# Strided attention output transposed per channel chunk and copied by ScalarE; strided jobs cut by slice halves; w_in issued behind batch 0's loads; attention steps at other places

## The chip, the cores and the metric

The kernel runs on one core of a Trainium2 chip. The metric is the time of one execution in microseconds (us) on the device. Engines are named as in the profile: PE is TensorE (PEld its weight loads), DVE VectorE, ACT ScalarE, POOL GpSimd, SP SyncE, whose queue issues most DMAs here.

## The reference

A sparse attention over 8 batches, 8 heads, 576 tokens and 64 channels, then a two-layer product with the Mish activation over all 4608 tokens.

```python
scores = q @ k^T / 8                       # per batch and head
heads 0..3: keys 0 to 31 places back       # "local"
heads 4..7: keys back in steps of 32       # "strided"
x = softmax(masked scores) @ v             # 4608 x 512, head by head in its columns
h = x @ w_in                               # 512 -> 2048
g = h * tanh(log(1 + exp(h)))              # Mish
out = g @ w_out                            # 2048 -> 512, float32
```

## The kernel before

**Layout of the attention.** Local heads work on six windows of 96 queries with 128 keys each. For strided heads a batch's tokens are laid out as 72 rows p of 8 slices j (token = 8p + j), so that a slice's 72 tokens hold all keys that its queries may see; a small mask, `stm`, selects them. After the products, x_l (local, 96 x 6 x 256) and x_s (strided, 72 x 8 x 256) are transposed on PE into xT, which has channels on partitions in four chunks of 128 (0 and 1 local, 2 and 3 strided) and the tokens of four batches in its columns, as a ring.

**Steps of a batch.** Eight t steps transpose q and k (`t_step`; each is 6 or 8 PE transposes into PSUM and one copy out, to qTs, kTs, qTl, kTl). Eight qk steps (`qk`, four strided and four local) put scores for two heads into the PSUM tile `ps`; ACT takes the exponential into a tile P, and POOL or DVE multiplies the mask on. Fourteen pv steps (`pv`, eight strided, one for each slice, six local, one for each window) multiply P with v for four heads into the PSUM tile `po`; DVE takes the reciprocal of the sums (`rden`) and multiplies it on, into x_s or x_l. Four xt steps (`xt`, two strided and two local) transpose x into the PSUM tile `trx` and copy it out to xT.

A strided qk job covers one head of each pair in all four slice pairs, so the first strided pv step needs all four jobs. A strided xt step covers two channel chunks and four slices; its copy reads PSUM in a row and writes xT in steps of eight elements (16 bytes), since the slices interleave in the token order. A local xt step covers two chunks and three windows and writes in a row.

**PSUM.** `ps_s` has one score tile in the block loop. `tr`, `po` and `trx` share two one-bank slots in turn (tag `pt`), so a step waits for the copy or product that empties the slot of the step before the last. `psh` and `pso` share two two-bank slots (`ps_mm`). A `pso` tile holds two output row groups, one in each bank; the first matmul of the second one waits until the first one is copied out to osb.

**The block loop.** Nine blocks t of 512 tokens. `mlp1` makes eight groups of h (16 matmuls into `psh`, then Mish on ACT into gT), with the t steps of batch t+1 between them. `mlp2` makes sixteen groups of the output (4 matmuls each; four row groups ot of four groups g4); behind group i stand the steps of entry i of the list that `attn_steps` returns, for batch t+1. In block 0 the groups run with g4 outside, so that w_out can arrive in quarters. Everything is issued in the order in which the code is written: there is no scheduler, and each engine and each DMA queue runs its own list from the front. After `mlp2`, POOL casts the inputs of batch t+2 to bf16, and SP loads those of batch t+3. Blocks 7 and 8 have no attention left.

**The start.** Batch 0's attention runs ahead of the loop. POOL issues the strided q and k loads and w_in in four parts; SP issues the local q and k and the values. `vl32` and the like are float32 landing tiles, vl, vs, kl, ql their bf16 copies.

## Time and profile before

| what | value |
|---|---|
| median of 3 runs | 424.3 us |
| the profiled execution: its own time, its span | 426.21 us, 424.4 us |
| mean granted clock of PE, as a share of 2.4 GHz | 0.943 |
| PE busy | 346.7 us, 82% of the span |
| DVE, ACT, POOL busy | 184.8, 144.7, 114.7 us |
| chain that ended last, share of the span | PE 63%, DVE 21%, ACT 8%, issue 4%, DMA 3% |
| mlp1 of block 0 begins | 46.92 us |
| block 3, from its first matmul to that of block 4 | 183.3 to 227.7 us |

Busy shares are means over stages that differ. In a row of the time order, "idle before" is how long the engine stood still ahead of that row, and the name behind the arrow is what released it. Ends of matmuls are modelled, so the starts of neighbouring rows tell more than the durations.

### The profile page before, as it was taken

The page shows a single profiled execution, that of the slowest core. Times are in us where ns is not written, and L with a number is a line of the kernel's source. Part 1 is how long each engine was busy: PE and PEld are TensorE (multiplying, and loading weights), DVE is VectorE, ACT ScalarE, POOL GpSimd, SP SyncE. Part 2 cuts the span into 40 slices and gives each one's busy share as a digit, 9 for nine tenths or more (in the row PEclk, how much of TensorE's full clock was granted, in tenths as well). Part 3 has the DMA queues.
Part 4 walks back from the last instruction along what each step waited for, and adds up shares of the span by engine and source line. Part 5 has one row for each costly group of instructions (what it writes and reads, how often), then busy time and mean ns, then how long its engine had stood idle before and what let it go on. Part 6 is the DMA issues. An engine that isn't in the chain of part 4 may idle for free.

```text
span 424.4 us, 6633 instructions
## 1 busy us (share of the span) xinstructions
PE 346.7 (82%) x2784; PEld 180.2 (42%) x2784; DVE 184.8 (44%) x390; ACT 144.7 (34%) x160; POOL 114.7 (27%) x105
## 2 busy tenths in 40 slices
PE   0334898779887989699869987898789888999995
PEld 0233354345443444355337934453445344444442
DVE  3174223772277226833493339523862377001011
ACT  1534255204530463045503551155106620520510
POOL 4159213801163105500470138002810230000000
PEclk9999999879996999799988999799969996999999
DMA  8999996019610791059014921190000010001001
GB/s 191 219 217 191 236 215 92 2 74 224 98 51 25 176 144 52 26 147 173 26 49 100 201 46 43 51 219 27 26 35 17 0 51 26 25 25 51 25 26 74
DMA packets 49389, 39.22 MB, mean 92 GB/s; under 512 B 27344, under 2 KB 42448, under 8 KB 49360
## 3 DMA queue, kind: packets, MB, share of 16 engines
q1 hardware_dynamic: 38736, 29.88, 30.1%
q0 software_dynamic: 10624, 8.92, 13.4%
q8 instruction: 22, 0.36, 0.4%
q14 instruction: 7, 0.06, 0.0%
HBM read 38.26 MB, written 9.44 MB: 112 GB/s over the span
## 4 chain that ended last, share of the span: by engine, by line
PE 63%; DVE 21%; ACT 8%; issue 4%; DMA 3%; SPq 1%; ACTq 0%
PE psh L290 28%; PE pso L305 25%; DVE xT L125 9%; DVE x_s L227 3%; DMA vs<-in_v_dram 3%; PE po L220 3%; DVE osb L311 3%; ACT P L203 3%; DVE P L204 2%; PE tr L154 2%; ACT L294 2%; PE trx L240 2%; DVE rden L226 2%; ACT gT L294 1%; ACT xT L123 1%
## 5 line engine op out<-in xcount | busy, mean ns | idle before, releaser
L305 PE MATMUL pso<-w_out,gT 128*128 128x512 bf16 x576 | 158.6, 408 | 9.4 <-DVE osb L311 9.4
L290 PE MATMUL psh<-xT,w_in 128*128 128x512 bf16 (+1 forms) x640 | 135.9, 362 | 2.2 <-ACT gT L294 1.7
L294 ACT ACTIVATE gT<-psh 128x1024 bf16<-128x1024 f32 x72 | 73.1, 1024 | 91.2 <-PE psh L290 91.2
L290 PEld LDWEIGHTS <-w_in 128*128 128x128 bf16 x640 | 60.7, 99 | 57.8 <-issue 6.4
L305 PEld LDWEIGHTS <-gT 128*128 128x128 bf16 x576 | 52.4, 103 | 60.3 <-issue 22.1
L311 DVE COPY osb<-pso 128x512 f32<-128x512 f32 x36 | 25.1, 697 | 66.6 <-PE pso L305 66.6
L203 ACT ACTIVATE P<-ps 72x576 bf16<-72x576 f32 (+1 forms) x64 | 41.0, 649 | 36.4 <-PE ps L185 25.7
L204 POOL TENSOR_TENSOR P<-P,stm 72x576 bf16<-72x576 bf16 x16 | 20.2, 1266 | 121.8 <-ACT P L203 121.8
L220 PEld LDWEIGHTS <-P 72*128 72x128 bf16 (+1 forms) x448 | 27.0, 108 | 51.9 <-issue 34.8
L125 DVE COPY xT<-trx 128x576 bf16<-128x576 bf16 x29 | 44.6, 1538 | 6.0 <-PE trx L240 6.0
L294 ACT ACT_TABLE_LOAD x8 | 10.3, 1283 | 101.8 <-PE psh L290 101.7
L220 PE MATMUL po<-vl,P 128*128 128x65 bf16 x192 | 16.8, 221 | 26.1 <-DVE rden L226 19.8
L204 POOL TENSOR_TENSOR P<-P,loc 128x576 bf16<-128x576 bf16 x23 | 29.6, 1291 | 25.3 <-ACT P L203 25.3
L226 DVE RECIPROCAL rden<-po 72x4 f32<-72x4 f32 (+1 forms) x112 | 22.0, 196 | 22.7 <-PE po L220 22.6
L227 DVE TENSOR_TENSOR x_s<-po,rden 72x256 bf16<-72x256 f32 x64 | 26.9, 421 | 2.2
L204 DVE TENSOR_TENSOR P<-P,stm 72x576 bf16<-72x576 bf16 x16 | 11.5, 725 | 31.9 <-ACT P L203 31.9
L125 DVE COPY kTs<-tr 128x576 bf16<-128x576 bf16 x16 | 7.3, 457 | 40.9 <-PE tr L145 40.9
L101 POOL DMA_DIRECT2D ks<-in_k_dram x8 | 6.3, 784 | 69.0 <-PE tr L145 68.1
L220 PE MATMUL po<-vs,P 72*128 72x65 bf16 x256 | 18.6, 202 | 5.2 <-DVE x_s L227 4.7
L227 DVE TENSOR_TENSOR x_l<-po,rden 96x256 bf16<-96x256 f32 x48 | 20.2, 421 | 1.9
L125 DVE COPY kTl<-tr 128x576 bf16<-128x576 bf16 x16 | 12.1, 758 | 20.3 <-PE tr L154 20.3
L196 PE MATMUL ps<-qTs,kTs 64*128 64x72 bf16 x256 | 10.0, 203 | 11.5 <-ACT P L203 11.1
(42 smaller groups left out, 214.2 us busy)
## 6 DMA issues: line engine op xcount, KB each, us to landing
out_dram<-osb SPq DMA_DIRECT2D x36, 256.0 KB, 2.0
vl<-in_v_dram SPq DMA_DIRECT2D x40, 128.0 KB, 10.9
kl<-in_k_dram SPq DMA_DIRECT2D x8, 576.0 KB, 5.2
ql<-in_q_dram SPq DMA_DIRECT2D x8, 576.0 KB, 7.3
vs<-in_v_dram SPq DMA_DIRECT2D x8, 576.0 KB
ks<-in_k_dram POOLq DMA_DIRECT2D x8, 288.0 KB, 10.0
qs<-in_q_dram POOLq DMA_DIRECT2D x8, 288.0 KB, 9.9
w_in<-in_moe_w_in_dram POOLq DMA_DIRECT2D x4, 512.0 KB, 17.7
```

Of the source, the lines that this page charges most:

```text
L125: eng.tensor_copy(out_, in_)
L154: nc.tensor.transpose(tr[:, PL * j:PL * j + PL], src[0:PL, j, 2 * hp:2 * hp + 2, :], ident[0:PL, 0:PL],)
L196: nc.tensor.matmul(ps[:, e, PN * u:PN * u + PN], lhsT=kTs[64 * e:64 * e + 64, c0:c0 + 128], rhs=qTs[64 * e:64 * e + 64, c0:c0 + PN], start ...
L203: nc.scalar.activation(pt[0:n, :, 0:288], ps[0:n, :, 0:288], AF.Exp, scale=scale)
L204: meng.tensor_tensor(out=pt[0:n, :, 0:288], in0=pt[0:n, :, 0:288], in1=mk.rearrange("p w c -> p (w c)").unsqueeze(1).to_broadcast([n, 2, 2 ...
L220: nc.tensor.matmul(po[:, h, :], lhsT=pt[0:n, c0:c0 + 128], rhs=rhs, start=True, stop=True,)
L226: nc.vector.reciprocal(rden[0:m, :], po[0:m, :, D])
L227: nc.vector.tensor_tensor(out=dst.rearrange("p (h d) -> p h d", h=4), in0=po[0:m, :, 0:D], in1=rden[0:m, :].unsqueeze(2).to_broadcast([m, ...
L290: nc.tensor.matmul(ps[:, u, o:o + n], lhsT=w_in[:, cc, fc * 128:(fc + 1) * 128], rhs=xT[:, cc, a:a + n], start=(cc == 0), stop=(cc == 3),)
L294: nc.scalar.activation(gT[:, 2 * g:2 * g + 2, :], ps[:], AF.Mish)
L305: nc.tensor.matmul(p[:, ot % 2, :], lhsT=gT[:, fc, 128 * ot:128 * ot + 128], rhs=w_out[:, fc, :], start=(fc == 0), stop=(fc == 15),)
L311: nc.vector.tensor_copy(osb[:], p[:, ot % 2, :])
```

## The change

- Strided jobs: a qk job now covers both heads of a pair in one half of the slices (c0 in `qk`; P's key and c0 in `pv`), so pv steps 0 to 3 need two jobs and steps 4 to 7 the other two.
- Strided xt: a step now takes one channel chunk and all eight slices. Its copy reads PSUM in steps of 72 elements and writes 576 elements of xT in a row.
- All xt copies and all output copies (osb) go to ACT; before, DVE made them, but for three of the xt copies of batch 0.
- `attn_steps`: an empty second entry; pv begins at entry 4 beside the last strided qk; xt("s") at 10 and 11, xt("l") at 13 and 15; the second local job's mask goes to POOL and the fourth's to DVE.
- The start: w_in is issued behind the cast of kl, which goes to POOL (ql's to DVE); vs is cast behind the exponentials; all four local masks go to POOL; the strided loads of batch 1 go behind batch 0's attention, its local and value loads behind a small DMA (`gate`) that reads slice 5 of x_s.

```diff
--- before.py
+++ after.py
@@ -76,6 +76,7 @@
     kTs = const.tile([128, 4 * 4 * PN + 64], BF16, name="kTs")
     NP = 8
     P = [const.tile([128, 2, 352], BF16, name=f"P{i}") for i in range(NP)]
+    gate = const.tile([1, 256], BF16, name="gate")
     x_l = const.tile([128, NW, 256], BF16, name="x_l")
     x_s = const.tile([128, CS, 256], BF16, name="x_s")
 
@@ -116,6 +117,13 @@
             nc.sync.dma_start(
                 vl32[:, i, :, :],
                 v[b, 0:4, WQ * i - 32:WQ * i + WQ, :].rearrange("h p d -> p h d"),
+            )
+
+    def load_w_in():
+        for c in range(4):
+            nc.gpsimd.dma_start(
+                w_in[:, :, 512 * c:512 * c + 512],
+                moe_w_in.rearrange("(cc p) f -> p cc f", p=128)[:, :, 512 * c:512 * c + 512],
             )
 
     def cast(eng, out_, in_):
@@ -191,7 +199,7 @@
                 n, mk = 128, loc[:, 3 * hf:3 * hf + 3, :]
             else:
                 for u in range(4):
-                    c0 = PN * (4 * (2 * hp + hf) + u)
+                    c0 = PN * (4 * (2 * hp + u // 2) + 2 * hf + u % 2)
                     for e in range(2):
                         nc.tensor.matmul(
                             ps[:, e, PN * u:PN * u + PN],
@@ -215,8 +223,9 @@
                     pt = self.P["l", h // 2, hf][:, h % 2]
                     n, m, c0, rhs = 128, WQ, WQ * w, vl[self.b % 2][:, i, h, :]
                 else:
-                    pt = self.P["s", h // 2, h % 2][:, i % 2]
-                    n, m, c0, rhs = PN, PN, PN * (i // 2), vs[self.b % 2][0:PN, h, i, :]
+                    pt = self.P["s", h // 2, i // 4][:, i % 2]
+                    n, m, c0 = PN, PN, PN * (2 * (h % 2) + i // 2 % 2)
+                    rhs = vs[self.b % 2][0:PN, h, i, :]
                 nc.tensor.matmul(
                     po[:, h, :], lhsT=pt[0:n, c0:c0 + 128], rhs=rhs,
                     start=True, stop=True,
@@ -230,28 +239,30 @@
             )
 
         def xt(self, kind, hf, eng=None):
-            eng = eng or nc.vector
+            eng = eng or nc.scalar
             tr = tile_t("trx")[:].bitcast(BF16)
-            nt, n = (3, WQ) if kind == "l" else (4, PN)
-            src = x_l if kind == "l" else x_s
-            for c in range(2):
-                for w in range(nt):
-                    o = (nt * c + w) * n
-                    nc.tensor.transpose(
-                        tr[:, o:o + n], src[0:n, nt * hf + w, 128 * c:128 * c + 128],
-                        ident[0:n, 0:n],
-                    )
             t0 = (self.b % RING) * S
             if kind == "l":
+                for c in range(2):
+                    for w in range(3):
+                        o = (3 * c + w) * WQ
+                        nc.tensor.transpose(
+                            tr[:, o:o + WQ], x_l[0:WQ, 3 * hf + w, 128 * c:128 * c + 128],
+                            ident[0:WQ, 0:WQ],
+                        )
                 cast(
                     eng, xT[:, 0:2, t0 + 288 * hf:t0 + 288 * hf + 288],
                     tr[:, 0:576].rearrange("p (c n) -> p c n", c=2),
                 )
             else:
-                dst = xT[:, 2:4, t0:t0 + S].rearrange("p c (n j) -> p c j n", j=CS)
+                for j in range(CS):
+                    nc.tensor.transpose(
+                        tr[:, PN * j:PN * j + PN], x_s[0:PN, j, 128 * hf:128 * hf + 128],
+                        ident[0:PN, 0:PN],
+                    )
                 cast(
-                    eng, dst[:, :, 4 * hf:4 * hf + 4, :],
-                    tr[:, 0:576].rearrange("p (c j n) -> p c j n", c=2, j=4),
+                    eng, xT[:, 2 + hf, t0:t0 + S].rearrange("p (n j) -> p n j", j=CS),
+                    tr[:, 0:576].rearrange("p (j n) -> p n j", j=CS),
                 )
 
     def attn_steps(b):
@@ -261,12 +272,12 @@
         V = lambda kd, i: (lambda: a.pv(kd, i))
         X = lambda kd, hf: (lambda: a.xt(kd, hf))
         return [
-            [Q("s", 0, 0, Po)], [Q("s", 1, 0, Dv)], [Q("s", 0, 1, Po)], [Q("s", 1, 1, Dv)],
-            [Q("l", 0, 0, Po), V("s", 0)], [Q("l", 1, 0, Dv), V("s", 1)],
-            [Q("l", 0, 1, Po), V("s", 2), V("s", 3)], [Q("l", 1, 1, Po), V("s", 4)],
-            [V("s", 5), V("s", 6)], [V("s", 7), X("s", 0)], [V("l", 0), V("l", 1)],
-            [V("l", 2), X("s", 1)], [V("l", 3), V("l", 4)], [V("l", 5), X("l", 0)],
-            [X("l", 1)], [],
+            [Q("s", 0, 0, Po)], [], [Q("s", 1, 0, Dv)], [Q("s", 0, 1, Po)],
+            [Q("s", 1, 1, Dv), V("s", 0)], [Q("l", 0, 0, Po), V("s", 1), V("s", 2)],
+            [Q("l", 1, 0, Po), V("s", 3)], [Q("l", 0, 1, Po), V("s", 4), V("s", 5)],
+            [Q("l", 1, 1, Dv), V("s", 6)], [V("s", 7)], [X("s", 0), V("l", 0)],
+            [X("s", 1), V("l", 1)], [V("l", 2)], [V("l", 3), V("l", 4), X("l", 0)],
+            [V("l", 5)], [X("l", 1)],
         ]
 
 
@@ -308,7 +319,7 @@
                 )
             if g4 == 3:
                 osb = o_pool.tile([128, DM], F32, tag="osb", name="osb")
-                nc.vector.tensor_copy(osb[:], p[:, ot % 2, :])
+                nc.scalar.copy(osb[:], p[:, ot % 2, :])
                 r = 512 * t + 128 * ot
                 nc.sync.dma_start(out[r:r + 128, :], osb[:])
         order = [(ot, g4) for ot in range(4) for g4 in range(4)]
@@ -325,11 +336,6 @@
         load_qk_loc(0)
         nc.sync.dma_start(loc[:], loc_h.ap())
         load_v(0)
-        for c in range(4):
-            nc.gpsimd.dma_start(
-                w_in[:, :, 512 * c:512 * c + 512],
-                moe_w_in.rearrange("(cc p) f -> p cc f", p=128)[:, :, 512 * c:512 * c + 512],
-            )
         Sc.preload_act_table(AF.Exp)
         Dv.memset(kTs[:, 16 * PN:16 * PN + 64], 0.0)
         Dv.memset(kTl[:, :, 0:32], 0.0)
@@ -341,36 +347,40 @@
             Dv.memset(P[i][:], 0.0)
 
         a = Attn(0)
-        for hp in range(2):
-            t_step(0, "s", "k", hp, Dv)
-            t_step(0, "s", "q", hp, Sc)
-        cast(Sc, vs[0][0:PN, :, :, 0:D], vs32[0:PN])
+        t_step(0, "s", "k", 0, Dv)
+        t_step(0, "s", "k", 1, Dv)
+        t_step(0, "s", "q", 0, Sc)
+        t_step(0, "s", "q", 1, Sc)
+        cast_qk_loc(0, Po, Dv)
+        load_w_in()
         a.qk("s", 0, 0, Po)
         a.qk("s", 1, 0, Dv, True)
         a.qk("s", 0, 1, Po, True)
         a.qk("s", 1, 1, Dv)
-        cast_qk_loc(0, Dv, Po)
+        cast(Sc, vs[0][0:PN, :, :, 0:D], vs32[0:PN])
         for i in range(0, NW, 3):
             cast(Po, vl[0][:, i:i + 3, :, 0:D], vl32[:, i:i + 3, :, :])
         for hp in range(2):
             t_step(0, "l", "k", hp, Dv)
             t_step(0, "l", "q", hp, Sc)
         a.qk("l", 0, 0, Po, True)
-        a.qk("l", 1, 0, Dv, True)
+        a.qk("l", 1, 0, Po, True)
         a.qk("l", 0, 1, Po)
-        a.qk("l", 1, 1, Dv, True)
-        load_qk_str(1)
+        a.qk("l", 1, 1, Po, True)
+        for j in range(8):
+            a.pv("s", j)
+        nc.sync.dma_start(gate[:], x_s[0:1, 5, :])
         load_qk_loc(1)
         load_v(1)
-        for j in range(8):
-            a.pv("s", j)
-        a.xt("s", 0, Sc)
-        a.xt("s", 1, Sc)
-        for i in range(6):
+        for i in range(3):
             a.pv("l", i)
-            if i == 3:
-                a.xt("l", 0, Sc)
-        a.xt("l", 1, Dv)
+        a.xt("s", 0)
+        a.xt("s", 1)
+        for i in range(3, 6):
+            a.pv("l", i)
+        a.xt("l", 0)
+        a.xt("l", 1)
+        load_qk_str(1)
         for c in range(4):
             nc.gpsimd.dma_start(
                 w_out[:, 4 * c:4 * c + 4, :],
```

ACT in block 1 (its last exponentials to the next Mish; P_88 to P_91 are local P tiles), before and then after:

```order
L203 ACTIVATE P_88<-ps 128x2x288
L203 ACTIVATE P_89<-ps 128x2x288
L203 ACTIVATE P_90<-ps 128x2x288
L203 ACTIVATE P_91<-ps 128x2x288
L294 ACT_TABLE_LOAD
L294 ACTIVATE gT<-psh 128x1024 x8
```

```order
L211 ACTIVATE P_89<-ps 128x2x288
L322 COPY osb<-pso 128x512
L211 ACTIVATE P_90<-ps 128x2x288
L211 ACTIVATE P_91<-ps 128x2x288
L131 COPY xT<-trx 128x576
L322 COPY osb<-pso 128x512
L131 COPY xT<-trx 128x576
L131 COPY xT<-trx 128x2x288
L322 COPY osb<-pso 128x512
L131 COPY xT<-trx 128x2x288
L305 ACT_TABLE_LOAD
L305 ACTIVATE gT<-psh 128x1024 x8
```

The four xT copies and the output copies of ot 1 to 3 now stand between the exponentials and Mish, the last xT copy behind the last output copy.

DVE at the same place, before (from the last strided pv step on) and then after (from the mask ahead of the last two on):

```order
L226 RECIPROCAL rden<-po 72x4
L227 TENSOR_TENSOR x_s<-po,rden 72x256
L125 COPY xT<-trx 128x2x4x72
L226 RECIPROCAL rden<-po 96x4
L227 TENSOR_TENSOR x_l<-po,rden 96x256
L226 RECIPROCAL rden<-po 96x4
L227 TENSOR_TENSOR x_l<-po,rden 96x256
L311 COPY osb<-pso 128x512
L226 RECIPROCAL rden<-po 96x4
L227 TENSOR_TENSOR x_l<-po,rden 96x256
L125 COPY xT<-trx 128x2x4x72
L226 RECIPROCAL rden<-po 96x4
```

```order
L212 TENSOR_TENSOR P_91<-P_91,loc 128x2x288
L235 RECIPROCAL rden<-po 72x4
L236 TENSOR_TENSOR x_s<-po,rden 72x256
L235 RECIPROCAL rden<-po 72x4
L236 TENSOR_TENSOR x_s<-po,rden 72x256
L235 RECIPROCAL rden<-po 96x4
L236 TENSOR_TENSOR x_l<-po,rden 96x256
L235 RECIPROCAL rden<-po 96x4
L236 TENSOR_TENSOR x_l<-po,rden 96x256
L235 RECIPROCAL rden<-po 96x4
```

The copies to xT and to osb have left DVE, and the mask of the last local job stands ahead of slice 6.

POOL at the start, from its first load on, before and then after:

```order
L101 DMA ks_74<-in_k_dram 72x4x512
L101 DMA qs_72<-in_q_dram 72x4x512
L329 DMA w_in<-in_moe_w_in_dram 128x4x512 x4
L204 ISA
L204 TENSOR_TENSOR P_84<-P_84,stm 72x2x288
L204 TENSOR_TENSOR P_86<-P_86,stm 72x2x288
L125 CAST ql_68<-ql_66 96x4x6x64
L125 CAST vl_76<-vl_64 128x12x64 x2
L204 TENSOR_TENSOR P_88<-P_88,loc 128x2x288
L204 TENSOR_TENSOR P_90<-P_90,loc 128x2x288
L101 DMA ks_75<-in_k_dram 72x4x512
L101 DMA qs_73<-in_q_dram 72x4x512
```

```order
L102 DMA ks_74<-in_k_dram 72x4x512
L102 DMA qs_72<-in_q_dram 72x4x512
L133 CAST kl_70<-kl_67 96x4x6x64
L124 DMA w_in<-in_moe_w_in_dram 128x4x512 x4
L212 ISA
L212 TENSOR_TENSOR P_84<-P_84,stm 72x2x288
L212 TENSOR_TENSOR P_86<-P_86,stm 72x2x288
L133 CAST vl_76<-vl_64 128x12x64 x2
L212 TENSOR_TENSOR P_88<-P_88,loc 128x2x288
L212 TENSOR_TENSOR P_89<-P_89,loc 128x2x288
L212 TENSOR_TENSOR P_90<-P_90,loc 128x2x288
L212 TENSOR_TENSOR P_91<-P_91,loc 128x2x288
```

w_in has moved behind the cast of kl, the cast of ql has gone, and there are four local masks instead of two ahead of the strided loads of batch 1.

## Rows read from the trace of the kernel before

**Rows 1.** windows in block 3: us, busy (xcount) by engine, PEclk, DMA share, GB/s:

```profile
199.40:227.50 28.10, 22.83 (x208) 11.17 (x205) 17.81 (x39) 7.43 (x10) 12.55 (x10) 0.88 0.13 39
206.00:212.60 6.60, 6.37 (x64) 2.89 (x64) 4.07 (x13) 2.74 (x5) 2.89 (x4) 1.00 0.12 42
212.60:217.50 4.90, 2.98 (x35) 1.72 (x33) 4.52 (x10) 0.00 (x0) 4.90 (x4) 1.00 0.14 54
219.40:225.80 6.40, 5.31 (x28) 2.64 (x28) 4.95 (x10) 0.00 (x0) 0.65 (x1) 0.50 0.11 41
```

**Rows 2.** time order, TensorE, same stage: start, us, op, [idle before, releaser]:

```profile
202.73 0.31 PE L196 MATMUL ps<-qTs,kTs 64*128 64x72 bf16 x8 [1.11 <-ACT P L203]
...
205.99 1.02 PE L305 MATMUL pso<-w_out,gT 128*128 128x512 bf16 x4 [0.55 <-DVE osb L311]
...
214.51 1.03 PE L305 MATMUL pso<-w_out,gT 128*128 128x512 bf16 x4
215.38 0.29 PE L220 MATMUL po<-vl,P 128*128 128x65 bf16 x4
217.49 0.29 PE L220 MATMUL po<-vl,P 128*128 128x65 bf16 x4 [1.82 <-DVE rden L226]
217.61 1.02 PE L305 MATMUL pso<-w_out,gT 128*128 128x512 bf16 x4
...
218.60 0.42 PE L240 MATMUL trx<-ident_sb,x_s 72*128 72x72 bf16 x8
219.42 1.86 PE L305 MATMUL pso<-w_out,gT 128*128 128x512 bf16 x4 [0.39 <-DVE osb L311]
221.08 0.42 PE L220 MATMUL po<-vl,P 128*128 128x65 bf16 x4
222.58 0.38 PE L220 MATMUL po<-vl,P 128*128 128x65 bf16 x4 [1.07 <-DVE rden L226]
```

**Rows 3.** time order, VectorE, same stage:

```profile
214.72 2.71 DVE L125 COPY xT<-trx 128x576 bf16<-128x576 bf16 x1
...
223.21 0.42 DVE L227 TENSOR_TENSOR x_l<-po,rden 96x256 bf16<-96x256 f32 x1
```

**Rows 4.** time order, ScalarE, ahead of block 0:

```profile
36.40 5.28 ACT L123 COPY xT<-trx 128x576 bf16<-128x576 bf16 x2 [6.20 <-PE trx L240]
```

**Rows 5.** groups by line and shape: busy us, mean ns of one, idle before:

```profile
L204 POOL TENSOR_TENSOR P<-P,loc 128x576 bf16<-128x576 bf16 x23 | 29.6, 1291 | 25.3 <-ACT P L203 25.3
...
L311 DVE COPY osb<-pso 128x512 f32<-128x512 f32 x36 | 25.1, 697 | 66.6 <-PE pso L305 66.6
...
L125 DVE COPY qTl<-tr 128x576 bf16<-128x576 bf16 x14 | 10.6, 756 | 14.8 <-PE tr L154 14.8
...
L125 DVE COPY qTs<-tr 128x576 bf16<-128x576 bf16 x14 | 6.4, 456 | 18.4 <-PE tr L145 18.4
...
L123 ACT COPY qTl<-tr 128x576 bf16<-128x576 bf16 x2 | 1.3, 640 | 5.9 <-PE tr L154 5.9
L123 ACT COPY qTs<-tr 128x576 bf16<-128x576 bf16 x2 | 1.3, 639 | 12.1 <-PE tr L145 12.1
```

**Rows 6.** time order, GpSimd, ahead of block 0:

```profile
2.92 3.01 POOL L329 DMA_DIRECT2D w_in<-in_moe_w_in_dram  x4
...
29.13 0.83 POOL L125 CAST vl<-vl 128x768 bf16<-128x768 f32 x1 [2.87 <-DMA vl<-in_v_dram]
29.92 2.92 POOL L204 TENSOR_TENSOR P<-P,loc 128x576 bf16<-128x576 bf16 x2
```

**Rows 7.** DMA queues from 16 to 18 us: packets, MB, share of 16 engines:

```profile
q0 software_dynamic: 314, 0.31, 90.9%
q1 hardware_dynamic: 314, 0.08, 29.8%
```

**Rows 8.** time order, TensorE, end of the start:

```profile
42.92 0.38 PE L220 MATMUL po<-vl,P 128*128 128x65 bf16 x4 [0.59 <-DVE rden L226]
...
46.92 11.19 PE L290 MATMUL psh<-xT,w_in 128*128 128x512 bf16 x40 [0.55 <-DVE xT L125]
```

## The prediction

> **What bounds the kernel now.** I read the busy shares and the chain of waits first: TensorE leads, and the chain runs through it, broken by VectorE copies. The kernel then falls into stages, so I cut one middle block (the fourth of nine, 183.3 to 227.7) by windows and read the second product's stage in order of time. Seven stages look alike: the second product of block t with the attention of batch t+1 between its groups. In the stage shown TensorE is busy 22.83 of 28.10 us and its granted clock averages 0.88 [rows 1]. The clock is at full level until 217.5, although there are waits before that, then at 0.50 (1.2 GHz) from 219.4 to 225.8; what stands ahead of the fall is a stretch with TensorE busy 2.98 of 4.90 us [rows 1]. So a wait costs twice there: its own length, and the half-speed matmuls behind it.
>
> The waits, by the starts of TensorE's neighbouring rows [rows 2]; a group of four output matmuls takes about 0.87 (214.51 to 215.38), one pv step 0.12 (217.49 to 217.61), one xt step about 0.27:
> - 202.73: the second strided qk step waits 1.11 for the first one's exponential, since there is one score buffer and that exponential stands behind a table load.
> - 205.99: 0.55 for the copy of the output tile's first half.
> - 217.49: local pv 1 comes 2.11 after local pv 0; less 0.13 that is 1.98 lost. Its PSUM slot is held by pv 0, whose reciprocal stands on VectorE behind the strided x copy, 2.71 long [rows 3].
> - 219.42: the group behind xt comes 0.55 late (218.60 + 0.27 = 218.87), for another output copy.
> - 222.58: pv comes 1.50 after the one before, 1.26 lost, behind the second strided copy.
> - Half clock: 5.31 busy us between 219.4 and 225.8 [rows 1] would be at most 2.65 shorter at full clock; I take 2.4, since the small matmuls there do not all halve.
> Sum per stage: 1.11 + 0.55 + 1.98 + 0.55 + 1.26 + 2.4 = 7.85.
>
> **The strided copy.** Before, one instruction took two channel chunks and half of the slices, and wrote every eighth element of xT: 2.71 on VectorE [rows 3], 5.28 for two, so 2.64, on ScalarE [rows 4]. Now one instruction takes one chunk and all eight slices, so it writes 576 elements in a row and the stepping is on the PSUM side. That pattern exists in the kernel before: the local q and k copies read PSUM in steps and write in a row. ScalarE takes 640 ns for one, against 639 ns for the strided q copy, which reads in a row; VectorE 756 against 456 [rows 5]. I take 0.64 on ScalarE, bounds 0.6 and 0.94 (0.64 and VectorE's 0.30 on top). The Trainium skill, SBUF — State Buffer, Door 1: The DMA port swizzle, speaks against the new direction: PSUM has 8-byte lines, and non-contiguous PSUM access slows matmuls significantly. It names matmuls; if it held for a copy as well, the sum would be that of the second rival instead of mine. The two ScalarE rows speak against that here, the two VectorE rows for a part of it.
>
> **The stage after, step by step.**
> - The empty second step puts one more group, 0.87, between the first two qk steps: of 1.11 some 0.25 stays.
> - Output copies go to ScalarE. 576 elements take it 0.64, so 512 take about 0.6 against 0.70 on VectorE [rows 5]. They stand in its queue between the exponentials, which come once per group; the first wait goes from 0.55 to 0.45.
> - xt("s", 0) now needs all eight slices, the last of them right ahead of it, and a mask on VectorE stands before slice 6. That is a wait of some 0.3; before, the same place has 0.3 for the last slice too. Nothing either way; if the mask comes late it could cost 0.5.
> - Behind xt("s", 0) TensorE has one pv (0.13) and one group (0.87) before xt("s", 1) wants the same PSUM slot. The copy of 0.64 with two hand-overs is done by then. The 1.98 goes to 0. VectorE holds only reciprocals and products there.
> - The third output copy stands in ScalarE's queue between the two xt copies. It starts at the end of its group, and the next group has xt (0.27) and pv (0.13) ahead of it: 0.7 less 0.4, some 0.3 to 0.4. I take 0.4 for 0.55.
> - The 1.26 goes, but xt("l", 0) now follows two pv steps in one step and takes the slot of the first. A pv holds its slot from 222.58 to 223.63, the end of its product [rows 2, 3], about 1.0; two pv steps cover 0.26. New wait: 0.75.
> - Clock: the longest wait left is 0.75, less than the 1.11 that passed at full clock. In 206.0 to 212.6, with small matmuls as dense, the clock stayed at 1.00 [rows 1]. I take full clock, with the fall as a rival.
> New waits 0.25 + 0.45 + 0.4 + 0.75 = 1.85. Gain 7.85 - 1.85 = 6.0 per stage, bounds 4.5 (each wait 0.3 longer) and 7.0. Seven stages: 42.
>
> **What the last step gives back.** xt("l", 1) now stands behind the last group, and the next block's first matmul reads what it writes where the tokens overlap: batch b's last 288 tokens begin at 576b + 288, block b ends at 512b + 512, so for b = 1, 2, 3. On ScalarE the last output copy stands ahead: 0.1 + 0.6 + 0.64 + 0.1, less the transposes' 0.27, some 1.2. Three times: 3.6. Bounds: 0, and seven times, 8.4, if the waits are coarser than the tokens.
>
> **The start.** mlp1 begins at 46.92 [rows 8]. Ahead of it the local values' second half lands at 29.13, GpSimd casts it, then masks [rows 6]. The change moves w_in's four issues (at 2.92 before) behind a cast on GpSimd. They stand in one queue behind ks and qs in any case, and each queue gets equal turns: 314 packets each in the two us from 16 to 18, in which the value load moves 0.08 MB and w_in 0.31 [rows 7]. So the later issue relieves the values only if it comes after qs is through; I take about the same landing, 29.1. Behind the cast, at 29.92, GpSimd now makes all four local masks, 1.29 each [rows 5]: 35.1. Strided pv and both strided copies are done by then: they no longer wait for a ScalarE cast ahead of the exponentials, and the copies cost 0.64, not 2.64. From pv 3 to mlp1 it took 46.92 - 42.92 = 4.0 [rows 8]; so mlp1 begins at about 39.1. Gain 7.7. Bounds: 3, if the loads land later than the casts want them; 15, if the values land at 21 and the chain of products alone decides. Behind it, w_out and batch 1 are issued about 2 us later and wanted 7.7 earlier. Block 0's second product takes w_out quarter by quarter over 28 us; I cost that at nothing, and at 3 (in the lower bound) if the last ones come late. The gate load puts batch 1's local loads behind slice 5, at about the time at which they were issued before.
>
> Transposes, qk and pv keep their counts; regrouping strided jobs by slice halves lets pv begin sooner and costs nothing by itself. The last two blocks have four waits on an output copy and one at the end, 0.1 shorter each: 0.4.
>
> **Sum.** 42 - 3.6 + 7.7 + 0.4 = 46.5. The profiled execution took 426.2 for a span of 424.4, so 379.7; the median, 424.3, is 1.9 below it: 377.8, say 378.
>
> **Rivals.** First, the clock still falls: small matmuls and five short waits suffice. For it: the fall before came in a stretch that had one long wait and many small matmuls, and the latter stay. Against: 206.0 to 212.6 at full clock [rows 1]. Price 2.4 x 7: 395. Second, the stepped PSUM read costs what the stepped write did, 2.64: then the slot is held 2.64 - 1.0 longer at xt("s", 1) and as long again at pv 2, some 3.5, and the clock falls as before, so that a stage gains nothing, the start some 5, and the last step still costs 3.6: about 422. Against it is the pair of 640 and 639 ns [rows 5]. Third, the start gains nothing, because w_in or the values land late: 378 + 7.7 = 386. Fourth, slower than before: the waits, now spread over the whole stage, bring the clock down at its beginning and hold it there. The sixteen groups alone would then take 13.9 longer, 16 x 0.87, in each of seven stages: 378 + 97 = 475. It turns slower from the point at which about half of the groups run at 1.2 GHz (46.5 of 97); the window at full clock that has a wait on either side speaks against it.
>
> **How the numbers follow.** Forecast (about 378) 0.62, clock falls late 0.15, start gains nothing 0.10, stepped PSUM read 0.05, clock down throughout 0.03; 0.05 for a wait that I don't see, mostly still faster. From 363 (7.0 per stage and 15 at the start, less 8) to 397 (clock rival and 2 more) holds 8 in 10. About 2% is what a measurement of this kernel tells from no change: faster by more 0.92, within it 0.05, slower 0.03.
>
> **What would show it.** The xT copies on ScalarE at 0.64 each; no wait over 0.8 in a stage; stages of about 22 and granted clock 1.00 in them; mlp1 at about 39; a wait of TensorE for the last xT copy of some 1.2 in blocks 1 to 3. Wrong would be: copies above 1.5, the clock at 0.50 inside the stages, or TensorE waiting for loads in blocks 0 and 1.

## The result, and the profile after

| what | before | after |
|---|---|---|
| median (424.91 and 379.15 are of the runs made side by side) | 424.91 us | 379.15 us |
| the profiled execution: its own time, its span | 426.21, 424.4 us | 381.16, 378.9 us |
| start, up to mlp1 of block 0 | 46.92 | 40.15 |
| block 0, mlp1 to mlp1 | 47.47 | 45.84 |
| blocks 1 and 2 | 44.35, 44.39 | 39.13, 39.13 |
| blocks 3 to 6 | 44.37, 44.45, 44.34, 44.34 | 37.96, 38.14, 37.96, 37.97 |
| block 7; block 8 to the end | 30.40; 33.37 | 29.43; 33.19 |

424.91 is the median of four executions, of which one took 1150.96 and the others 424.01 to 425.53; the ratio leaves that one out. The ratio is 0.8925, 95% interval [0.8846, 0.9004]: faster, by 45.5 us between the two spans. The block rows are differences between the first `psh` rows of neighbouring blocks in the time order, so they add up to the spans (block 3 of the kernel before runs from 183.13 to 227.50 by these rows, not from 183.3 to 227.7). They say at once where to look: four blocks alike, two that are longer by 1.2 and one by 8, and a start that gained 6.8. Block 4 is 0.1 to 0.2 longer than its neighbours because its tokens wrap round the ring: a group of h has 16 matmuls of 256 columns there, and 8 of 512 in the other blocks.

Four blocks alike first. This is TensorE's time order in block 4, its waits only; they answer to [rows 2]:

```profile
221.62 0.31 PE L204 MATMUL ps<-qTs,kTs 64*128 64x72 bf16 x8 [0.24 <-ACT P L211]
...
223.61 1.02 PE L316 MATMUL pso<-w_out,gT 128*128 128x512 bf16 x4 [0.48 <-ACT osb L322]
...
226.65 0.30 PE L229 MATMUL po<-vs,P 72*128 72x65 bf16 x4 [0.23 <-DVE x_s L236]
...
235.09 1.02 PE L316 MATMUL pso<-w_out,gT 128*128 128x512 bf16 x4 [0.33 <-ACT osb L322]
...
237.97 0.43 PE L249 MATMUL trx<-ident_sb,x_l 96*128 96x96 bf16 x6 [0.60 <-DVE x_l L236]
```

Five waits of 0.23 to 0.60 stand where 0.55 to 1.98 stood; the one of 0.23, for the slot of the strided products, stood in the kernel before as well (0.23 at 210.36). The windows of the same stage (first line, against the first of [rows 1]) and of two stretches of block 0:

```profile
218.40:240.50 22.10, 20.18 (x206) 10.09 (x204) 10.06 (x32) 10.85 (x17) 12.78 (x10) 1.00 0.23 55
71.00:75.50 4.50, 2.05 (x23) 1.08 (x21) 3.97 (x5) 0.14 (x1) 4.50 (x3) 0.96 0.01 3
75.50:78.00 2.50, 2.50 (x18) 1.31 (x16) 0.61 (x3) 0.73 (x2) 1.75 (x3) 0.50 0.03 7
```

In the stage TensorE is busy 20.18 of 22.10 us, at full clock. Before, it was 22.83 of 28.10 at 0.88. Block 0 still has the old picture, a hole (2.05 busy of 4.50) and then half clock; we come back to it. The copies, from the groups by form (busy us, mean ns, idle before), and two of them in ScalarE's time order in block 4, a strided one (for L259's transposes) and a local one (for L249's):

```profile
L322 ACT COPY osb<-pso 128x512 f32<-128x512 f32 x36 | 21.1, 585 | 43.7 <-PE pso L316 43.7
...
L131 ACT COPY xT<-trx 128x576 bf16<-128x576 bf16 x32 | 20.4, 641 | 50.4 <-PE trx L259 30.7 <-PE trx L249 19.6
...
L212 DVE TENSOR_TENSOR P<-P,loc 128x576 bf16<-128x576 bf16 x7 | 5.9, 841 | 5.2 <-ACT P L211 5.2
...
233.42 0.64 ACT L131 COPY xT<-trx 128x576 bf16<-128x576 bf16 x1 [1.90 <-PE trx L259]
...
238.43 0.64 ACT L131 COPY xT<-trx 128x576 bf16<-128x576 bf16 x1 [2.85 <-PE trx L249]
```

All 32 copies to xT take 641 ns in the mean, and the ones with the stepped PSUM read take no longer than the others, against 2.71 us and 5.28 for two before [rows 3, 4]. The output copy takes 585 on ScalarE, 697 on VectorE [rows 5]. The last row has a mean of 841 for seven masks; six of them take about 0.48 and one 2.99. Means of small groups hide such a thing, which is why one goes back to the time order. First matmuls of blocks 0, 1, 3 and 4, TensorE's time order:

```profile
40.15 1.44 PE L301 MATMUL psh<-xT,w_in 128*128 128x512 bf16 x3 [0.73 <-ACT xT L131]
...
85.99 1.24 PE L301 MATMUL psh<-xT,w_in 128*128 128x512 bf16 x5 [1.00 <-ACT xT L131]
...
164.25 1.89 PE L301 MATMUL psh<-xT,w_in 128*128 128x512 bf16 x8 [1.00 <-ACT xT L131]
...
202.21 1.91 PE L301 MATMUL psh<-xT,w_in 128*128 128x256 bf16 x16
```

Blocks 1 to 3 wait 1.00 for the last xT copy, block 4 and later ones don't wait. ScalarE's time order at the start of block 1 has the reason, the last output copy ahead of it:

```profile
84.81 0.58 ACT L322 COPY osb<-pso 128x512 f32<-128x512 f32 x1 [1.16 <-PE pso L316]
85.29 0.65 ACT L131 COPY xT<-trx 128x576 bf16<-128x576 bf16 x1
```

And block 0, where 4 us were lost. VectorE, then GpSimd, then TensorE, time order:

```profile
70.96 2.99 DVE L212 TENSOR_TENSOR P<-P,loc 128x576 bf16<-128x576 bf16 x1 [0.79 <-ACT P L211]
...
68.23 2.60 POOL L212 TENSOR_TENSOR P<-P,loc 128x576 bf16<-128x576 bf16 x2 [0.60 <-ACT P L211]
70.77 1.46 POOL L133 CAST kl<-kl 96x1536 bf16<-96x1536 f32 x1
72.18 1.46 POOL L133 CAST ql<-ql 96x1536 bf16<-96x1536 f32 x1
...
74.56 0.77 PE L259 MATMUL trx<-ident_sb,x_s 72*128 72x72 bf16 x8 [2.30 <-DVE x_s L236]
```

The mask begins 0.19 after a cast on GpSimd and ends 0.3 after the next cast, which follows without a gap. The products of slices 6 and 7 stand behind it on VectorE, so TensorE waits 2.30, and its granted clock is 0.50 in the window behind (75.50 to 78.00). In block 1 the order is the other way round, the mask 0.12 ahead of the cast (VectorE, GpSimd):

```profile
115.16 0.48 DVE L212 TENSOR_TENSOR P<-P,loc 128x576 bf16<-128x576 bf16 x1 [0.73 <-ACT P L211]
...
115.28 1.69 POOL L133 CAST kl<-kl 96x1536 bf16<-96x1536 f32 x1
```

There the mask takes 0.48 and the cast 1.69 instead of 1.46. At the start, GpSimd:

```profile
8.39 3.01 POOL L124 DMA_DIRECT2D w_in<-in_moe_w_in_dram  x4
...
30.23 0.83 POOL L133 CAST vl<-vl 128x768 bf16<-128x768 f32 x1 [4.50 <-DMA vl<-in_v_dram]
31.01 4.96 POOL L212 TENSOR_TENSOR P<-P,loc 128x576 bf16<-128x576 bf16 x4
```

The second half of the local values landed at 30.23, with w_in issued 5.5 us later; before it was 29.13 [rows 6].

### The profile page after: what moved, and what is told of

It reads as the page before. It is cut to its first block, busy times and chain, and to the rows that moved or that the text cites. A ratio compares the mean times of both kernels' runs of the same rounds, so it can differ in the third digit from the quotient of the medians.

```text
span 378.9 us, 6623 instructions
## 1 busy us (share of the span) xinstructions
PE 328.1 (87%) x2784; PEld 172.6 (46%) x2784; DVE 118.3 (31%) x323; ACT 178.0 (47%) x225; POOL 118.0 (31%) x107
## 4 chain that ended last, share of the span: by engine, by line
PE 75%; ACT 7%; DVE 5%; SPq 4%; issue 4%; DMA 3%; POOL 1%; ACTq 0%; POOLq 0%
PE psh L301 34%; PE pso L316 29%; SPq L117 4%; ACT osb L322 3%; PE po L229 3%; DMA vl<-in_v_dram 3%; ACT P L211 3%; PE tr L153 2%; PE tr L162 2%; DVE P L212 2%; PE ps L204 2%; PE ps L193 1%; DVE x_l L236 1%; PE trx L249 1%; PE trx L259 1%
## 5 line engine op out<-in xcount | busy, mean ns | idle before, releaser
L316 PE MATMUL pso<-w_out,gT 128*128 128x512 bf16 x576 | 143.2, 381 | 8.8 <-ACT osb L322 8.8
L316 PEld LDWEIGHTS <-gT 128*128 128x128 bf16 x576 | 50.1, 98 | 55.4 <-issue 11.7
L131 ACT COPY xT<-trx 128x576 bf16<-128x576 bf16 x32 | 20.4, 641 | 50.4 <-PE trx L259 30.7
L322 ACT COPY osb<-pso 128x512 f32<-128x512 f32 x36 | 21.1, 585 | 43.7 <-PE pso L316 43.7
L212 POOL TENSOR_TENSOR P<-P,loc 128x576 bf16<-128x576 bf16 x25 | 31.7, 1272 | 16.6 <-ACT P L211 16.5
L229 PEld LDWEIGHTS <-P 72*128 72x128 bf16 (+1 forms) x448 | 22.8, 102 | 23.4 <-POOL P L212 7.7
L235 DVE RECIPROCAL rden<-po 72x4 f32<-72x4 f32 (+1 forms) x112 | 19.5, 174 | 44.1 <-PE po L229 44.1
L229 PE MATMUL po<-vl,P 128*128 128x65 bf16 x192 | 13.7, 202 | 8.4 <-POOL P L212 7.4
L133 POOL CAST vl<-vl 128x768 bf16<-128x768 f32 x16 | 12.9, 826 | 15.0 <-DMA vl<-in_v_dram 15.0
L133 DVE COPY qTl<-tr 128x576 bf16<-128x576 bf16 x14 | 10.6, 756 | 14.8 <-PE tr L162 14.8
```

Of the source, the lines that this page charges most:

```text
L131: nc.scalar.copy(out_, in_)
L133: eng.tensor_copy(out_, in_)
L212: meng.tensor_tensor(out=pt[0:n, :, 0:288], in0=pt[0:n, :, 0:288], in1=mk.rearrange("p w c -> p (w c)").unsqueeze(1).to_broadcast([n, 2, 2 ...
L229: nc.tensor.matmul(po[:, h, :], lhsT=pt[0:n, c0:c0 + 128], rhs=rhs, start=True, stop=True,)
L235: nc.vector.reciprocal(rden[0:m, :], po[0:m, :, D])
L316: nc.tensor.matmul(p[:, ot % 2, :], lhsT=gT[:, fc, 128 * ot:128 * ot + 128], rhs=w_out[:, fc, :], start=(fc == 0), stop=(fc == 15),)
```

## The experiments

My theory was that the gain comes from the direction of the strided copy, and the rest from where copies and steps stand. The rivals: the new direction is as dear as the old one and something else pays; the copies' move to ScalarE pays; the spacing of the steps pays. Times are medians; each ratio is to the kernel before, run beside it.

**Direction alone.** The kernel before with the new strided `xt` only, copies left on VectorE:

```diff
-                dst = xT[:, 2:4, t0:t0 + S].rearrange("p c (n j) -> p c j n", j=CS)
+                for j in range(CS):
+                    nc.tensor.transpose(
+                        tr[:, PN * j:PN * j + PN], x_s[0:PN, j, 128 * hf:128 * hf + 128],
+                        ident[0:PN, 0:PN],
+                    )
                 cast(
-                    eng, dst[:, :, 4 * hf:4 * hf + 4, :],
-                    tr[:, 0:576].rearrange("p (c j n) -> p c j n", c=2, j=4),
+                    eng, xT[:, 2 + hf, t0:t0 + S].rearrange("p (n j) -> p n j", j=CS),
+                    tr[:, 0:576].rearrange("p (j n) -> p n j", j=CS),
```

> The kernel before with one part of the change alone: strided xt by channel chunk, its copy writing xT in a row; copies stay on VectorE, steps and start as before. Theory A (the gain comes from the copy's write in a row: 0.76 on VectorE for 2.7, so the slot and the reciprocals come free and the clock stays up): a stage loses some 3.2 of its 7.85, so 4.6 x 7 and 4 at the start, about 388 us, granted clock 0.99 or more. Theory B (it comes from ScalarE taking the copies off VectorE) and theory C (it comes from the new places of the steps): above 412 us, clock still at 0.95.

386.53 us, 0.9119 [0.9096, 0.9142], granted clock 0.999. xT copies on VectorE take 596 ns in the mean, which hides two lengths (VectorE in block 4, a strided copy and a local one):

```profile
233.94 0.76 DVE L125 COPY xT<-trx 128x576 bf16<-128x576 bf16 x1 [0.30 <-PE trx L250]
...
239.85 0.44 DVE L125 COPY xT<-trx 128x576 bf16<-128x576 bf16 x1
```

So on VectorE the stepped PSUM read costs 0.30, as the pair of 756 and 456 ns [rows 5] had it, and on ScalarE nothing. Blocks 1 to 6 take 39.44 to 39.61. This part alone brings 40.2 of the 45.5 us between the spans; its block 0, 41.32, does not have the loss of about 4 that the whole change has there.

**The rest without it.** The changed kernel, with the copy stepping on the write side again (one chunk, eight slices):

```diff
-                    eng, xT[:, 2 + hf, t0:t0 + S].rearrange("p (n j) -> p n j", j=CS),
-                    tr[:, 0:576].rearrange("p (j n) -> p n j", j=CS),
+                    eng, xT[:, 2 + hf, t0:t0 + S].rearrange("p (n j) -> p j n", j=CS),
+                    tr[:, 0:576].rearrange("p (j n) -> p j n", j=CS),
```

> The changed kernel with its strided xT copy turned round: PSUM read in a row, xT written in steps of eight elements, still on ScalarE, all else kept. Theory A: the copy takes 2.6, the slot waits behind xt come back (some 3.5 a stage), the clock falls again (2.4 a stage), the start loses 3: 421 us (415 to 427). Theories B and C: below 395 us, since ScalarE is free there and VectorE's queue holds no copy.

425.66 us, 1.004 [1.0011, 1.0069], clock 0.928. The xT group and TensorE's waits in one stage:

```profile
L131 ACT COPY xT<-trx 128x576 bf16<-128x576 bf16 x32 | 53.5, 1690 | 55.9 <-PE trx L259 29.8 <-PE trx L249 25.6
...
219.94 0.42 PE L259 MATMUL trx<-ident_sb,x_s 72*128 72x72 bf16 x8 [1.82 <-ACT xT L131]
...
223.16 0.38 PE L229 MATMUL po<-vl,P 128*128 128x65 bf16 x4 [1.77 <-ACT xT L131]
```

With half the copies at 0.64, the strided half takes 2.70 (53.5 less 16 x 0.64, over 16). TensorE waits for the slot at the two places that the second rival named, 3.59 in sum against its 3.5. Without the direction, everything else in the change brings nothing in sum: the start is 2.7 earlier (44.27), and blocks 0 and 1 are 2.7 and 2.6 longer than in the kernel before (50.19 and 46.94). It is the direction, shown from both sides.

**Copies back on VectorE.** xT and output copies of the changed kernel:

```diff
-            eng = eng or nc.scalar
+            eng = eng or nc.vector
-                nc.scalar.copy(osb[:], p[:, ot % 2, :])
+                nc.vector.tensor_copy(osb[:], p[:, ot % 2, :])
```

> The changed kernel with all xT copies and the output copies back on VectorE. Theory A: 0.76 a strided copy and 0.70 an output copy, each 0.1 longer, and reciprocals behind them: 380 to 388 us, clock 0.99 or more. Theory B: above 405 us.

405.39 us, 0.9556 [0.952, 0.9591], clock 0.974. My number was missed, and the time is the one at which ScalarE would be the point of the change. The trace says otherwise (VectorE in blocks 1 and 6, GpSimd and TensorE in block 1):

```profile
117.60 3.05 DVE L212 TENSOR_TENSOR P<-P,loc 128x576 bf16<-128x576 bf16 x1 [0.59 <-ACT P L211]
...
331.45 0.46 DVE L212 TENSOR_TENSOR P<-P,loc 128x576 bf16<-128x576 bf16 x1 [0.59 <-ACT P L211]
...
117.47 1.46 POOL L133 CAST kl<-kl 96x1536 bf16<-96x1536 f32 x1
118.88 1.46 POOL L133 CAST ql<-ql 96x1536 bf16<-96x1536 f32 x1
...
121.25 0.75 PE L259 MATMUL trx<-ident_sb,x_s 72*128 72x72 bf16 x8 [2.30 <-DVE x_s L236]
```

The mask now comes a little later and falls behind GpSimd's cast in every block but the last of the seven, which has no casts behind it (331.45, 0.46). That block takes 38.85, blocks 1 to 5 take 42.14 to 43.51. That made a theory to test: the casts lock the mask out. Two runs did that. One puts this mask on GpSimd:

```diff
-            [Q("l", 1, 1, Dv), V("s", 6)], [V("s", 7)], [X("s", 0), V("l", 0)],
+            [Q("l", 1, 1, Po), V("s", 6)], [V("s", 7)], [X("s", 0), V("l", 0)],
```

> The changed kernel with the xT and output copies back on VectorE, and the last local mask on GpSimd. If that kernel's 405.4 us came from the mask that is locked out behind GpSimd's casts (one wait of TensorE of 2.3 and a clock fall in every block): about 383 us, granted clock 0.99 or more, no wait of TensorE over 1.0 in a stage. If it came from the copies themselves, which stand in VectorE's queue ahead of reciprocals and products: still over 400 us with the clock at 0.97 or less.

382.68 us, 0.9027 [0.8992, 0.9062], clock 0.996. The other leaves it on VectorE and holds back the casts alone:

```diff
             if t + 2 < B:
+                Po.tensor_copy(gate[0:1, 0:8], P[7][0:1, 0, 0:8])
                 cast_qk_loc(t + 2, Po, Po)
```

> The kernel with the copies on VectorE and the last local mask on VectorE too (405.4 us), with one edit: a copy of 8 elements of that mask's tile on GpSimd stands ahead of GpSimd's casts, so that these begin only when the mask is through. Nothing else is moved. If the mask takes 3.05 instead of 0.46 because GpSimd's cast begins just before it and the next cast follows without a gap: the mask 0.5 or less in all seven blocks, TensorE's wait for x_s under 1.0, about 383 us with the clock at 0.99 or more. If VectorE is only too full in that kernel, or the mask is slow for another reason: 404 us or more, the mask still over 2.

385.43 us, 0.9075 [0.9027, 0.9122], clock 1.000. VectorE and GpSimd in block 1:

```profile
113.08 0.46 DVE L212 TENSOR_TENSOR P<-P,loc 128x576 bf16<-128x576 bf16 x1 [0.65 <-ACT P L211]
...
113.60 0.18 POOL L415 COPY gate<-P 1x8 bf16<-1x8 bf16 x1 [0.65 <-DVE P L212]
113.73 1.45 POOL L133 CAST kl<-kl 96x1536 bf16<-96x1536 f32 x1
```

All seven masks take 0.46. One small copy that sets the order of two engines is worth 20 us in that kernel. What the copies' engine is worth is then read between equals: with the last mask on GpSimd, 382.68 on VectorE against 375.28 on ScalarE (below). By the first `psh` and `pso` rows of this pair's blocks, 2.6 of these 7.4 lie in the first products of blocks 2 to 7; the part on the prediction says more of them.

**That mask on GpSimd in the changed kernel.** The same one-word edit:

> The changed kernel with the mask of the last local job on GpSimd in every block. Theory F (in block 0 that mask takes 2.99 us on VectorE because GpSimd's casts run just then, TensorE waits 2.3 for it and the clock falls once): block 0 takes 42 instead of 45.8, granted clock 1.00, 375 to 376.5 us, and less spread between executions. Rival (block 0 is longer because its output groups run in another order): no change, 379 us.

375.28 us, 0.8863 [0.8826, 0.8899], clock 0.999. Block 0 takes 41.64 instead of 45.84; the 2.30 is gone. By the medians alone it isn't told apart from the change: the intervals overlap. The four runs of the changed kernel have mean clocks of 0.995 to 1.000 and times of 376.5 to 381.2, so the fall in block 0 need not come in every execution, and the profile shown is of the slowest. The block times tell it, together with the kernel that issues w_in first (below), where the mask stays on VectorE and costs less.

**The old list of steps** in the changed kernel, the whole list of before; its beginning and end:

```diff
-            [Q("s", 0, 0, Po)], [], [Q("s", 1, 0, Dv)], [Q("s", 0, 1, Po)],
...
-            [V("l", 5)], [X("l", 1)],
+            [Q("s", 0, 0, Po)], [Q("s", 1, 0, Dv)], [Q("s", 0, 1, Po)], [Q("s", 1, 1, Dv)],
...
+            [X("l", 1)], [],
```

The last local mask is on GpSimd in it, the second on VectorE.

> The changed kernel with the list of attention steps of the kernel before. Theory A: the first qk wait is 0.87 longer and the first strided xt stands in one entry with the last strided pv, 0.9 more; the last xT copy comes earlier (1.2 back in three blocks): about 1.5 x 7 less 3.6, so 384 to 394 us. Theory C: above 405 us.

379.80 us, 0.8958 [0.8935, 0.898]. I had it dearer. Blocks 3 to 6 take 38.85 to 39.01, 0.9 more than after; blocks 1 and 2 38.88, 0.25 less; block 0 41.46, 4.4 less. So re-spacing pays 0.9 in a stage, and the change gave all of it back at the block starts and in block 0. Against the last kernel, which has its mask on GpSimd too, the spans differ by 4.2: that is what the spacing is worth where nothing is in its way.

**The old start**, order and engines of the kernel before ahead of the loop, w_in's issue included:

```diff
-        cast_qk_loc(0, Po, Dv)
-        load_w_in()
...
-        a.qk("l", 1, 0, Po, True)
+        a.qk("l", 1, 0, Dv, True)
         a.qk("l", 0, 1, Po)
-        a.qk("l", 1, 1, Po, True)
...
+        a.qk("l", 1, 1, Dv, True)
+        load_qk_str(1)
```

> The changed kernel with the start of the kernel before (order of loads, casts, masks and steps ahead of block 0), xT copies at their new places and direction. Theory A (4 of the 6.8 us that the start gained are the two strided copies, 2.64 down to 0.64 each; the new order gives the rest): mlp1 begins at 43, about 382 us. Theory D (the new order of loads, casts and masks gives all of it): mlp1 at 46.5, about 386 us.

383.06 us, 0.9045 [0.9013, 0.9077]; mlp1 at 42.09. So 4.8 of the start's 6.8 come from the shorter copy alone (46.92 to 42.09; direction alone has 42.12), 1.9 from the new order.

**w_in ahead again**, its issue back in its old place:

```diff
         load_v(0)
+        load_w_in()
...
         cast_qk_loc(0, Po, Dv)
-        load_w_in()
```

> The changed kernel with w_in issued at its old place, ahead of everything but the strided loads. Theory A (w_in stands behind ks and qs in one queue, and the queues take equal turns, so that its issue time hardly moves the values): mlp1 begins within 1 us of 40.2, 378 to 380 us. Theory E (the late issue relieves batch 0's loads): values land 3 us or more later, 382 us or more.

376.27 us, 0.8888 [0.884, 0.8935]; mlp1 at 38.38, the values' cast at 28.46. Not slower, and in the profile 1.8 earlier: issuing w_in late gains nothing. Block 0 of this kernel takes 43.59. Its steps there are those of the changed kernel, but the mask waits for one cast only (VectorE, then GpSimd):

```profile
69.98 1.58 DVE L212 TENSOR_TENSOR P<-P,loc 128x576 bf16<-128x576 bf16 x1 [0.79 <-ACT P L211]
...
69.79 1.46 POOL L133 CAST kl<-kl 96x1536 bf16<-96x1536 f32 x1
71.20 1.69 POOL L133 CAST ql<-ql 96x1536 bf16<-96x1536 f32 x1
```

TensorE waits 0.89 for x_s and its clock stays at 1.00 in block 0. The mask begins 0.19 behind the first cast as in the changed kernel; what decides between one cast and two, no run shows. So the mask on VectorE costs block 0 between 2.0 (43.59 against 41.64) and 4.2 (45.84), 0.2 of it as in every other block.

**Local masks ahead of the values' casts** on GpSimd:

```diff
-        for i in range(0, NW, 3):
-            cast(Po, vl[0][:, i:i + 3, :, 0:D], vl32[:, i:i + 3, :, :])
         for hp in range(2):
...
         a.qk("l", 1, 1, Po, True)
+        for i in range(0, NW, 3):
+            cast(Po, vl[0][:, i:i + 3, :, 0:D], vl32[:, i:i + 3, :, :])
```

> The changed kernel with batch 0's four local masks ahead of the casts of its values on GpSimd. Theory G (TensorE's 6.5 us wait at the start is for masks that stand behind a cast that waits for the values): the masks are done before the values land, mlp1 begins at about 35 to 36, 374 to 375.5 us. Rival (the loads set the start and what follows): mlp1 earlier by 2 us at most, or block 0 waits for weights or for batch 1 and the time stays at 378 or more.

377.13 us, 0.8893 [0.8855, 0.8931]: no gain that can be told, although mlp1 begins at 34.73, 5.4 earlier. Block 0 takes 47.25 then. GpSimd and TensorE there:

```profile
56.88 0.97 POOL L133 CAST vl<-vl 128x768 bf16<-128x768 f32 x1 [8.50 <-DMA vl<-in_v_dram]
...
60.67 2.52 POOL L212 TENSOR_TENSOR P<-P,stm 72x576 bf16<-72x576 bf16 x2
...
62.03 0.32 PE L229 MATMUL po<-vs,P 72*128 72x65 bf16 x4 [3.62 <-POOL P L212]
```

GpSimd's queue stands 8.50 at the cast of batch 1's values, and batch 1's masks stand behind it. Is it the load, or the place of the cast? The last two runs answer that, together with the waits at the end of a stage. First the local xt steps a group or more earlier, mask on GpSimd:

```diff
-            [X("s", 1), V("l", 1)], [V("l", 2)], [V("l", 3), V("l", 4), X("l", 0)],
-            [V("l", 5)], [X("l", 1)],
+            [X("s", 1), V("l", 1)], [V("l", 2), V("l", 3)], [V("l", 4), V("l", 5)],
+            [X("l", 0), X("l", 1)], [],
```

> The changed kernel with the last local mask on GpSimd and both local xt steps a group or more earlier, so that the last entry of the list is empty. If TensorE's waits at the end of a stage are prices of these two places (0.6 for x_l in seven blocks, 1.0 for the last xT copy behind the last output copy at the start of blocks 1 to 3): 375.3 - 4.2 - 3.0, about 368 us. If the waits only move to other steps, because two local pv steps now stand in one entry: 374 to 376 us.

368.25 us, 0.8673 [0.8649, 0.8697], clock 1.000. The 1.00 at the starts of blocks 1 to 3 and the 0.60 are gone, and nothing came in their place: blocks 1 and 2 take 37.61, blocks 3 to 6 37.30 to 37.46. Block 0 takes 38.76, 2.9 less than with the mask alone; 2.15 of those are the two waits and one of 0.55 for an output copy.

Then with the masks first at the start, and batch 1's local values cast in block 0 behind its second strided mask:

```diff
-        cast_v(1, Po, Po)
+        cast(Po, vs[1][0:PN, :, :, 0:D], vs32[0:PN])
...
-        load_v(2)
...
+                if t == 0 and i == 3:
+                    for j in range(0, NW, 3):
+                        cast(Po, vl[1][:, j:j + 3, :, 0:D], vl32[:, j:j + 3, :, :])
+                    load_v(2)
```

> As the last one, and at the start the four local masks ahead of the casts of the local values, and the casts of batch 1's local values moved into block 0's second product, behind its second strided mask. If what block 0 gave back in the kernel with the masks first was only GpSimd's queue (its masks of batch 1 behind a cast that waits for batch 1's values): 5.4 us less than the last one at mlp1 of block 0 and kept at the start of block 1, so about 363 us. If the loads themselves decide: block 0 longer by what the start gains, and the total within 1 us of the last one.

363.59 us, 0.8569 [0.8526, 0.8611]. mlp1 begins at 35.01, 4.84 earlier than in the run before, and block 0 takes 39.71, 0.95 longer: 3.9 are kept. It was the queue, then, for most of it; of the 0.95, 0.76 is a longer wait of TensorE (1.01 instead of 0.25) for the second strided mask on VectorE, which now runs beside the moved casts and takes 1.25 instead of 0.48. This version beats both kernels.

## Why the prediction held, step by step

The forecast was 378 in 363 to 397; 379.15 came. The mechanism was right: the copy's direction, the waits that it takes away, the clock. That the sum is right to 1 us (46.5 foretold, 45.5 between the spans) is luck, because terms that were off by up to 3.5 cancel. The lower end of the range isn't what its terms give: 49 + 15 + 0.4 less 8 is 56.4, which makes 368; 363 comes out with 3.6 for the last step.

- **Copy.** 0.64 taken, 0.641 measured. The pair of 640 and 639 ns [rows 5] was the row to go by. The Trainium skill's rule that non-contiguous PSUM access slows matmuls (SBUF — State Buffer, Door 1: The DMA port swizzle) doesn't carry over to a ScalarE copy here; a VectorE copy pays 0.30. The second rival falls with it, and the run with the stepped write shows that it had the right place and price for the case that it described.
- **Stage.** 1.11, 1.98, 1.26 and the two output waits went, or shrank as said. New waits, in the order of the text: 0.25, 0.45, 0.4 and 0.75 foretold, 0.24, 0.48, 0.33 and 0.60 measured. From its first `pso` row to the end of the block, the second product of block 3 went from 28.12 to 22.06: 6.06, foretold 6.0. The clock stayed at 1.00 in the stages of blocks 1 to 6, so the first rival falls there; in block 0 the clock did fall to 0.50, one of the prediction's own signs of being wrong, for the reason below.
- **First product.** The blocks gained 6.31 to 6.41, more than their second products, because the first products of blocks 2 to 6 became 0.35 shorter (16.25 to 15.90 in block 3), and that of block 7 0.84. The prediction had this at nothing, without a reason. The rows of ScalarE at the start of block 7, before (block start 360.63) and after (316.28):

```profile
362.61 1.28 ACT L294 ACT_TABLE_LOAD   x1 [16.94 <-PE psh L290]
...
317.41 1.28 ACT L305 ACT_TABLE_LOAD   x1
```

Before, the table load begins 1.98 into the block, when the first group of h is through, and TensorE then waits about 0.2 for a Mish in blocks 2 to 6 and 0.72 in block 7. After, it begins 1.13 into the block, straight behind the last xT copy, and these waits are gone. Of all kernels here, those with the copies on VectorE have the late load and the wait, and those with the copies on ScalarE have neither. Why the load waits for the group in the one queue and not in the other stays open.

- **Last step.** 1.2 in blocks 1 to 3 foretold from the token ranges; a wait of 1.00 came in just these, and 1.17 between the block rows.
- **Start.** 7.7 foretold, 6.77 measured. The mis-sized term is the landing of the values, taken as 29.1 and measured 30.23; mlp1 is 1.05 later than foretold and the landing 1.1. The rest of that chain, four masks and 4.0 behind, came as worked out (4.96 and 4.2).
- **Block 0** is the step that failed. "If the mask comes late it could cost 0.5", the text says of the one on VectorE before slice 6: in the profile it cost about 4, 2.30 of waiting and the half clock behind it. I had asked what is queued behind the mask on VectorE, and not what GpSimd does at that moment. The runs with the mask on GpSimd and with the casts held back show the cause. The trace of the kernel before had a small case of it, a local mask that begins 0.03 after GpSimd's cast at 29.13 [rows 6] and takes 1.11, where those in its block loop take 0.46:

```profile
29.16 1.11 DVE L204 TENSOR_TENSOR P<-P,loc 128x576 bf16<-128x576 bf16 x1 [1.55 <-ACT P L203]
```

- **Last blocks.** 0.4 foretold, 1.15 measured: four output waits of 0.72 instead of 0.78, and in block 7 the wait of 0.72 for a Mish that is no longer there.

Sum of the misses: second products of blocks 1 to 6 with the last step +0.6, first products of blocks 0 to 6 +2.1, last blocks +0.75, start -0.9, second product of block 0 -3.5, which is -1.0.

Left open: how far the order of issue moves the landing of the values. In the ten profiles with w_in issued late the cast of their second half begins at 29.35 to 30.51, in the four with w_in first at 28.46 to 29.68. So the late issue relieves nothing; whether it costs the 0.9 between the two means, these few profiles can't tell.

## What to carry to other kernels

Where a copy between PSUM and SBUF must step, let it step on the PSUM side and write in a row, as here, and look for a pair of rows in the kernel's own trace that prices it on the engine that will do it. When work is moved to an engine, look at what its neighbour does in that microsecond: a VectorE product of two SBUF operands beside back-to-back work on GpSimd can take six times its length. A tiny copy that makes the neighbour wait for the product, or giving the product to the neighbour itself, takes that away. A gain at the start is kept only if the queues behind it (here GpSimd's casts of the next batch) aren't waiting for loads; and a step whose result opens the next block belongs a group ahead of the last copy on its engine.

## What the runs showed of the hardware

A VectorE product of two SBUF operands (128 x 576) takes 0.46 to 0.48. If a GpSimd cast began 0.12 to 0.19 before it and another one follows without a gap, it takes 2.99 to 3.06 in nine blocks of four kernels and 1.58 or 1.59 in one block each of two others: it ends about 0.3 after the second cast, or after the first. The Trainium skill, SBUF — State Buffer, Who interferes with whom, says that such an instruction contends with a GpSimd one that reads SBUF, and that the order of issue decides which of the two blocks. The trace agrees (mask first: 0.48, and the cast 1.69 instead of 1.46). For how many GpSimd instructions in a row the blocked one waits, that section doesn't say; here it was two, or one.

With 576 bf16 elements on each of 128 partitions, a stepped write into SBUF costs ScalarE 2.70 (steps of 16 bytes), a stepped read of the same elements from PSUM 0.64, no more than a read in a row; VectorE takes 0.76 for that read and 0.44 for the local copy. A mean clock of 0.995 hid a fall to 0.50 that lasted at least 2.5 us.
